# New times in the tables that order every engine's queue, and a head-by-head layout for the first pair

## The chip, the cores and the metric

The kernel runs on one core of one Trainium2 chip. The metric is the time of one launch in microseconds on the device; the time of a kernel is the median of its runs. The profile is of one execution of its own.

## The reference

Two batches of 8 heads, 768 positions, 64 wide. Each position of q and k is assigned to one of 16 clusters of its head, and attention goes only to keys of the query's own cluster. The result, 1536 tokens by 512, goes through two MLP layers of 512 to 2048 to 512.

```python
q_assign = np.argmax(np.einsum('bhsd,hcd->bhsc', q_n, c_n), axis=-1)
k_assign = np.argmax(np.einsum('bhsd,hcd->bhsc', k_n, c_n), axis=-1)
mask = q_assign[:, :, :, None] == k_assign[:, :, None, :]
scores = np.where(mask, scale * np.matmul(q, k.transpose(0, 1, 3, 2)), -1000000000.0)
...
x = softmax(scores) @ v, heads side by side as 512 columns
h = x @ w_in;  g = h * np.cos(h);  x = g @ w_out
h = x @ w_in2; g = np.where(h > 0, h, np.exp(np.minimum(h, 0)) - 1); x = g @ w_out2
```

q_n, k_n and c_n are the rows divided by their norms. q, k, v and the centroids are float32, the weights of the MLPs are float64.

## The kernel before

**Staging.** The 16 heads are worked on in eight pairs, pp = 0 to 7. A pair has 12 steps, one for each block of 128 queries of one head, 96 steps in all. In a step, qk (L741, L744) multiplies one block of queries with all 768 keys. Each operand is split into a rounded high part and the rest (low part); both are stacked along the contracted dimension in tiles X0, X1, and a second product, with the tiles T0, T1, adds the remaining term of the split together with the mask in 16 further rows, which come from Z. rowmax (L749, DVE) takes the row maximum, expo (L757, ACT) the exponential, turn (L766, PE) transposes it in six blocks, p_hi (L780, ACT) and p_lo (L786, DVE) split it, and av (L797, PE) multiplies it with the values. x_low, x_main (L839, L850, ACT) and x_add (L858, POOL) put the result into X; recip_rows and recip_out (L817, L823) send the reciprocal row sums through DRAM with DMAs on SP, and x_mul (L864, POOL) multiplies by them.

**What a pair needs before its steps.** load_nat (L300 to L319) loads k, q and v from DRAM on SP's queue: 192 KB for each head of k and q (two buffers each), 384 KB for v of both heads (one buffer). raw_pe (L436) transposes, raw_out, raw_copy and raw_low (L445 to L462) split into high and low, stack (L473 to L478) copies these with six DMAs on SP into X0, X1, T0 and T1. square and sum_sq (L530 to L552) give the squared norms, norm_seed and norm_step the norms by Newton steps, sims_pe (L581, PE) the similarities with the centroids, sims_add (L588, DVE) and sims_scale, sims_max, sims_eq, sims_first, best and assign (L601 to L647) the cluster of each position, mask_pe (L655) and mask_out (L667 to L683) the rows of the mask, which four DMAs on SP bring from the tile Z into T0 and T1 of k and q. values_hi (L699) and values_lo (L708), on POOL, split v. For the first pair first_pe, first_hi, first_low and first_hi2 (L490 to L519) stand in place of raw and stack, and norm_steps (L361 to L370, eleven small operations on DVE) in place of norm_step.

**The MLPs.** A block is (m, t, f): layer m, 512 tokens t of 3, 128 of the 2048 hidden columns f. load_w (L105 to L120) brings the weights of one f into a slot with two DMAs, w_part (L122 to L150) turns the float64 words into a rounded high part and a low part: part 0 on ACT (L133, u), part 1 a shift on DVE (L135), part 2 an or with the low word on DVE (L137), part 4 on ACT (L142), part 5 a subtract on POOL (L148). x_hi, x_lo (L171, L179) split the input tokens, g1 (L198) is the first product, act (L215 to L240) the activation in eight parts (in layer 1 with ACT's Sin at L224, the product on DVE at L226 and the low part GL on POOL at L240), g2 (L257) the second product into four accumulators, finish (L268 to L274) copies the four into X or into o, from where an output DMA goes (L278). open_mlp closes the pool of the pairs' tiles and opens the first five weight slots, close_attention opens the others.

**What sets the order.** The tables at L26 to L33 give every part a time in steps: FIRST for the first pair, PAIR for a pair before its steps (its zero is the first step of the pair ahead), STEP, HALF and UNIT for what belongs to a step, to three steps, to six; LAST for the change from attention to layer 1; MLP for blocks. All parts are collected, sorted by time, and issued in that order inside one manual schedule:

```python
with tc.manual_schedule():
    for time, _, part, args in sorted(items, key=lambda a: a[:2]):
        part(*args)
```

So each engine, and SP's queue of DMAs, runs its own instructions in the order of these times; between engines only data and free buffers are waited for. The numbers matter only through the order that they give.

Of the kernel before, what the change touches and what calls it, by code (L numbers as in the profile page):

```python
# [8 lines left out]
F32 = mybir.dt.float32  # L9
# [5 lines left out]
AF = mybir.ActivationFunctionType  # L15
ALU = mybir.AluOpType
# [24 lines left out]
SS_ON = {'k': 'pool', 'q': 'pool'}  # L41
# [13 lines left out]
def kernel(ctx: ExitStack, tc: tile.TileContext, q, k, v, centroids,  # L55
# [225 lines left out]
    with ExitStack() as actx:  # L281
# [23 lines left out]
        def load_nat(pp, which, js=(0, 1)):  # L305
            b, hp = divmod(pp, NP)
            src = {"q": q, "k": k, "v": v}[which]
            if which == "v":
                t = nat.tile([128, 2, C, D], F32, tag=which, name="nat_v")
                nats[pp, which] = t  # L310
                nc.sync.dma_start(out=t, in_=src[b, 2 * hp:2 * hp + 2].rearrange("h (p c) d -> p h c d", c=C))
            else:
                if js[0] == 0:
                    nats[pp, which] = nat.tile([128, C, 2, D], F32, tag=which, bufs=2, name=f"nat_{which}")
                for j in js:
                    nc.sync.dma_start(out=nats[pp, which][:, :, j, :],
                                      in_=src[b, 2 * hp + j].rearrange("(p c) d -> p c d", c=C))
# [688 lines left out]
```

## Time and profile before

| | us |
|---|---|
| runs | 842.17, 837.16, 836.62 |
| median of the runs | 837.16 |
| profiled execution | 839.53 |
| its span (first to last instruction) | 836.7 |
| PE busy | 790.7 |
| DVE busy | 514.2 |
| ACT busy | 484.2 |
| POOL busy | 408.5 |

The engines are PE (TensorE), DVE (VectorE), ACT (ScalarE), POOL (GpSimd) and SP, which here only issues DMAs. In a list of instructions each line has the start and the length in microseconds, the engine, the line of the kernel, the operation, the tile written and the tiles read, and in square brackets how long the engine had stood idle and what ended that: the engine, tile and line of the instruction, or the DMA. An xN behind the tile is the number of equal instructions in a row that the line stands for. PEclk is the TensorE clock that was granted, as a share of its full 2.4 GHz.

### The profile page before, as it was taken

Reading aid. Unit: us, or ns where it says so; the run is one execution under the profiler, and the core shown is the slowest. Engines: PE = TensorE matmul, PEld = TensorE weight load, DVE = VectorE, ACT = ScalarE, POOL = GpSimd, SP = SyncE. Lnnn points to the kernel's source line nnn. Section 1 sums busy time; section 2 is a strip of 40 time slices with the busy share of each in tenths; the row PEclk is TensorE's granted clock in tenths of the full one; section 3 lists DMA queues with packets and bytes.
Section 4 is the critical chain, followed back from the end, with each engine's and each line's share of the span. In section 5 each row is a group of like instructions: output and inputs, shape, how many; then the busy total and the mean of one; then the engine's idle time right before and its main releaser. Section 6 shows DMA issues by size and latency. Waiting matters only on the chain.

```text
span 836.7 us, 11270 instructions
## 1 busy us (share of the span) xinstructions
PE 790.7 (94%) x4003; PEld 671.1 (80%) x4003; DVE 514.2 (61%) x766; ACT 484.2 (58%) x894; POOL 408.5 (49%) x426
## 2 busy tenths in 40 slices
PE   5789999999998898989999999998998999999998
PEld 4689989998897686768888888876886888888886
DVE  7978998988987989985445445596675111121110
ACT  4568988988987966764333443447454333343232
POOL 3546676666662685772223222278878322212221
PEclk9689999999999999999999999999999999999999
DMA  5447467457347196000000045452000100000001
GB/s 115 106 74 165 93 141 177 88 134 171 76 97 262 18 319 243 1 0 1 1 0 1 1 152 201 155 201 97 1 1 0 51 1 0 1 36 16 0 1 50
DMA packets 65479, 67.98 MB, mean 81 GB/s; under 512 B 33488, under 2 KB 53968, under 8 KB 65424
## 3 DMA queue, kind: packets, MB, share of 16 engines
q1 hardware_dynamic: 65424, 67.28, 29.7%
q8 instruction: 31, 0.51, 0.3%
q14 instruction: 24, 0.20, 0.1%
HBM read 46.17 MB, written 3.19 MB: 59 GB/s over the span
## 4 chain that ended last, share of the span: by engine, by line
PE 58%; DVE 19%; ACT 6%; DMA 6%; POOL 6%; issue 4%; SPq 1%; POOLq 0%; ACTq 0%
PE a L257 23%; PE h L198 22%; DVE u L137 4%; PE pt L766 4%; PE px L797 3%; DVE PL L786 2%; DVE m L749 2%; POOL slot L148 2%; DMA raw<-in_moe_w_out_dram 2%; DVE u L135 2%; ACT u L133 2%; PE pt_sim L581 2%; PE s L741 2%; PE s L744 1%; DMA X1q<-lo 1%
## 5 line engine op out<-in xcount | busy, mean ns | idle before, releaser
L240 POOL TENSOR_TENSOR GL<-A,GH 128x512 fp32r<-128x512 f32 x96 | 137.1, 1428 | 279.7 <-ACT GH L235 258.8
L198 PE MATMUL h<-XH,slot 128*128 128x512 f32 x768 | 250.8, 390 | 4.3 <-POOL slot L148 4.3
L198 PEld LDWEIGHTS h<-XH,slot 128*128 128x128 f32 x768 | 144.0, 188 | 36.4 <-POOL slot L148 6.6
L198 PE MATMUL h<-XL,slot 128*128 128x512 f32 x384 | 150.0, 391 | 1.6 <-DVE XL L179 1.5
L257 PE MATMUL a<-GH,slot 128*128 128x512 f32 x384 | 125.2, 390 | 0.0
L232 DVE SCALAR_TENSOR_TENSOR A<-R,h 128x512 f32<-128x512 f32 x48 | 32.8, 684 | 145.3 <-ACT R L230 121.0
L257 PE MATMUL a<-slot,GH 128*128 128x512 f32 x384 | 119.3, 392 | 2.0 <-DVE X L270 1.9
L786 DVE TENSOR_TENSOR PL<-pt,PH 128x384 fp32r<-128x384 f32 x192 | 99.6, 550 | 19.8 <-ACT PH L780 18.3
L780 ACT ACTIVATE PH<-pt 128x384 fp32r<-128x384 f32 x192 | 87.4, 502 | 24.2 <-PE pt L766 23.8
L766 PE MATMUL pt<-ident,P 128*128 128x128 f32 x576 | 89.9, 283 | 6.7 <-DVE PL L786 3.7
L749 DVE TENSOR_REDUCE m<-s 128x1 f32<-128x768 f32 x96 | 90.8, 946 | 6.2 <-PE s L744 4.8
L757 ACT ACTIVATE P<-s,m 128x768 f32<-128x768 f32 x96 | 88.1, 918 | 7.1 <-DVE m L749 6.3
L148 POOL TENSOR_TENSOR slot<-u,slot 128x1024 fp32r<-128x1024 f32 x32 | 82.9, 2591 | 12.8 <-ACT slot L142 12.7
L257 PEld LDWEIGHTS a<-slot,GH 128*128 128x128 f32 x384 | 72.4, 189 | 17.7 <-DVE X L270 2.4
L198 PEld LDWEIGHTS h<-XL,slot 128*128 128x128 f32 x384 | 72.2, 188 | 17.7 <-DVE XL L179 2.8
L228 ACT ACTIVATE R<-h 128x512 f32<-128x512 f32 x48 | 28.4, 592 | 99.4 <-PE h L198 99.4
L257 PEld LDWEIGHTS a<-GH,slot 128*128 128x128 f32 x384 | 72.1, 188 | 15.4 <-DVE A L226 0.4
L766 PEld LDWEIGHTS pt<-ident,P 128*128 128x128 f32 x576 | 68.9, 144 | 13.8 <-DVE PL L786 6.1
L257 PE MATMUL a<-GL,slot 128*128 128x512 f32 x192 | 75.5, 393 | 3.6 <-POOL GL L240 3.6
L257 PE MATMUL a<-slot,GL 128*128 128x512 f32 x192 | 75.4, 393 | 0.7 <-POOL GL L240 0.7
L137 DVE SCALAR_TENSOR_TENSOR u<-raw,u 128x1024 uint32<-128x1024 uint32 x32 | 70.3, 2198 | 0.7
L235 ACT ACTIVATE GH<-A 128x512 fp32r<-128x512 f32 x80 | 50.1, 627 | 34.1 <-DVE A L226 24.5
(139 smaller groups left out, 1271.6 us busy)
## 6 DMA issues: line engine op xcount, KB each, us to landing
raw<-in_moe_w_in_dram SPq DMA_DIRECT2D x32, 512.0 KB, 6.1
raw<-in_moe_w_out_dram SPq DMA_DIRECT2D x32, 512.0 KB, 6.9
nat_k<-in_k_dram SPq DMA_DIRECT2D x16, 192.0 KB, 5.1
nat_q<-in_q_dram SPq DMA_DIRECT2D x16, 192.0 KB, 4.6
nat_v<-in_v_dram SPq DMA_DIRECT2D x8, 384.0 KB, 4.7
R<-row SPq DMA_DIRECT2D x32, 96.0 KB, 3.5
out_dram<-o SPq DMA_DIRECT2D x12, 256.0 KB, 2.0
X0k<-hi SPq DMA_DIRECT2D x7, 192.0 KB, 2.6
```

The lines of the kernel that those rows point to most:

```text
L137: nc.vector.scalar_tensor_tensor(out=u, in0=low, scalar=29, in1=u, op0=ALU.logical_shift_right, op1=ALU.bitwise_or)
L148: eng.tensor_tensor(out=lo, in0=f32(w_u[m, f]), in1=f32(hi), op=ALU.subtract)
L198: nc.tensor.matmul(h, lhsT=a[:, kd, :], rhs=b, start=(kd == 0 and i == 0), stop=(kd == NKD - 1 and i == 2))
L232: nc.vector.scalar_tensor_tensor(out=A, in0=R, scalar=-1.0, in1=h, op0=ALU.add, op1=ALU.max)
L235: nc.scalar.activation(out=GH, in_=A, func=AF.Copy)
L240: eng.tensor_tensor(out=GL, in0=A, in1=f32(GH), op=ALU.subtract)
L257: nc.tensor.matmul(accs[m, t][e], lhsT=a, rhs=b, start=(f == 0 and i == 0), stop=(f == NF - 1 and i == 2))
L749: nc.vector.tensor_reduce(out=m, in_=st[n]["s"][:, :, 0:HW], axis=AX.XY, op=ALU.max, negate=True)
L757: nc.scalar.activation(out=P, in_=st[n]["s"][:, :, 0:HW], func=AF.Exp, bias=st[n]["m"], accum_out=dens[u][:, j, r:r + 1])
L766: nc.tensor.transpose(pt[:, c * 128:(c + 1) * 128], st[n]["P"][:, e, c * 128:(c + 1) * 128], ident)
L780: nc.scalar.activation(out=ph, in_=pt, func=AF.Copy)
L786: nc.vector.tensor_tensor(out=pl, in0=pt, in1=f32(ph), op=ALU.subtract)
```

## The change

All the tables have new times, and with them most engines' queues have another order in places. Where the prediction speaks of an order, these entries are the ones (the tables are printed here with one entry to a line, the others left out):

```diff
 # FIRST, second dict (head 1 of the first pair)
-    'norm_steps': 0.7914,
+    'norm_steps': 1.525,
-    'sims_add:q': 0.7934,
+    'sims_add:q': 1.382,
-    'square:k': -1.0086,
+    'square:k': -20.284,
-    'sum_sq:k': -0.2561,
+    'sum_sq:k': -7.354,
-    'mask_pe': 3.8836,
+    'mask_pe': 3.799,
-    'mask_out:q': 4.085,
+    'mask_out:q': 4.427,
-    'values_lo': 2.8339,
+    'values_lo': 7.012,
...
 # PAIR
-    'raw_low:k:1': 1.5691,
+    'raw_low:k:1': 1.368,
-    'raw_pe:q:0': 2.675,
+    'raw_pe:q:0': 2.135,
-    'raw_low:q:1': 3.6687,
+    'raw_low:q:1': 4.213,
-    'stack:k': 2.2827,
+    'stack:k': 3.051,
-    'stack:q': 3.6861,
+    'stack:q': 5.0,
-    'load_nat:k': -3.9551,
+    'load_nat:k': -6.192,
-    'load_nat:q': -15.9556,
+    'load_nat:q': -0.577,
-    'load_nat:v': 8.0349,
+    'load_nat:v': -4.693,
-    'sims_pe:q:5': 5.677,
+    'sims_pe:q:5': 6.327,
-    'sims_pe:q:8': 6.6344,
+    'sims_pe:q:8': 6.039,
-    'values_lo:0': 11.4018,
+    'values_lo:0': 10.555,
-    'values_lo:1': 11.4113,
+    'values_lo:1': 9.536,
-    'mask_out': 9.2034,
+    'mask_out': 9.035,
...
 # UNIT
-    'recip_rows': 3.9065,
+    'recip_rows': 8.839,
-    'recip_out': 5.8425,
+    'recip_out': 9.063,
-    'x_add': 8.9091,
+    'x_add': 9.736,
-    'x_mul': 9.3379,
+    'x_mul': 13.628,
...
 # LAST
-    'open_mlp': (-12.2667,),
+    'open_mlp': (-11.915,),
-    'w_part:0': (-10.2061, -10.1596, -9.4684, -6.9746, -4.7605, -1.9051),
+    'w_part:0': (-9.3, -8.885, -8.673, -6.449, -5.648, -4.914),
-    'w_part:1': (-4.9214, -4.7585, -4.4517, -3.4424, -1.5263, 0.943),
+    'w_part:1': (-8.986, -7.104, -5.724, -3.249, -2.53, -2.367),
-    'g1': (2.0747, 2.3775, 5.2068, 5.8432),
+    'g1': (0.671, 1.959, 4.434, 5.707),
-    'close_attention': (5.9122,),
+    'close_attention': (6.221,),
...
 # MLP, first dict (layer 1)
-    'g2': 4.2196,
+    'g2': 4.6,
-    'late_g2:14': -0.193,
+    'late_g2:14': -0.733,
-    'finish:0': 5.1961,
+    'finish:0': 4.599,
-    'finish:1': 5.1941,
+    'finish:1': 4.016,
-    'finish:2': 4.5732,
+    'finish:2': 4.59,
-    'finish:3': 5.4814,
+    'finish:3': 4.616,
...
 # MLP, second dict (layer 2)
-    'g1': 0.8646,
+    'g1': 0.31,
-    'x_hi:0': 0.3601,
+    'x_hi:0': 1.072,
-    'x_hi:1': 0.8015,
+    'x_hi:1': 1.123,
-    'x_hi:2': 0.5952,
+    'x_hi:2': 1.51,
-    'x_hi:3': 0.5932,
+    'x_hi:3': 1.828,
-    'finish:0': 4.5752,
+    'finish:0': 4.121,
-    'finish:1': 4.7174,
+    'finish:1': 5.137,
-    'finish:2': 4.7389,
+    'finish:2': 6.206,
-    'finish:3': 5.0175,
+    'finish:3': 6.165,
...
```

Below the tables, the first pair's k and q lie in SBUF head by head, [128, 2, C, D], so that the rows of one head are 6 x 64 elements without a gap; the later pairs keep [128, C, 2, D] and are read through a rearranged view. The tile of the squares is [128, 2, C, D] for all pairs. No instruction is added or removed.

```diff
@@ -311,9 +311,10 @@
                 nc.sync.dma_start(out=t, in_=src[b, 2 * hp:2 * hp + 2].rearrange("h (p c) d -> p h c d", c=C))
             else:
                 if js[0] == 0:
-                    nats[pp, which] = nat.tile([128, C, 2, D], F32, tag=which, bufs=2, name=f"nat_{which}")
+                    t = nat.tile([128, C, 2, D] if pp else [128, 2, C, D], F32, tag=which, bufs=2, name=f"nat_{which}")
+                    nats[pp, which] = t.rearrange("p c h d -> p h c d") if pp else t
                 for j in js:
-                    nc.sync.dma_start(out=nats[pp, which][:, :, j, :],
+                    nc.sync.dma_start(out=nats[pp, which][:, j],
                                       in_=src[b, 2 * hp + j].rearrange("(p c) d -> p c d", c=C))
             for j in js:
                 made("nat", pp, which, j)
@@ -434,7 +435,7 @@
             pt = raw_pt[pp, w, half] = pt_tile("pt_raw")
             for c in range(HC):
                 nc.tensor.transpose(pt[:, c * 128:(c + 1) * 128],
-                                    t[:, half * HC + c].rearrange("p h d -> p (h d)"), ident)
+                                    t[:, :, half * HC + c].rearrange("p h d -> p (h d)"), ident)
 
         raws_sb = {}
 
@@ -487,7 +488,7 @@
             raw_pt[0, w, j] = ps
             for c in range(C):
                 o = (c % HC) * 128
-                nc.tensor.transpose(ps[0:64, c // HC, o:o + 128], nats[0, w][:, c, j, :], ident)
+                nc.tensor.transpose(ps[0:64, c // HC, o:o + 128], nats[0, w][:, j, c, :], ident)
 
         def first_parts(w, j):
             rows = lambda t, upper: (t[64:128] if upper else t[0:64]).rearrange("p (e n) -> p e n", e=2)
@@ -529,12 +530,12 @@
 
         def square(pp, w, js):
             need(*[("nat", pp, w, j) for j in js])
-            t = nats[pp, w][:, :, cols(js)]
-            sq = pre.tile([128, C, 2, D], F32, tag="sq", bufs=2, name="sq")
+            t = nats[pp, w][:, cols(js)]
+            sq = pre.tile([128, 2, C, D], F32, tag="sq", bufs=2, name="sq")
             if pp == 0 and SQ0_ON[w, js[0]] == "act":
-                nc.scalar.activation(out=sq[:, :, cols(js)], in_=t, func=AF.Square)
+                nc.scalar.activation(out=sq[:, cols(js)], in_=t, func=AF.Square)
             elif pp == 0:
-                nc.gpsimd.tensor_tensor(out=sq[:, :, cols(js)], in0=t, in1=t, op=ALU.mult)
+                nc.gpsimd.tensor_tensor(out=sq[:, cols(js)], in0=t, in1=t, op=ALU.mult)
             else:
                 nc.gpsimd.tensor_tensor(out=sq, in0=t, in1=t, op=ALU.mult)
             if pp > 0 and SS_ON[w] == "pool":
@@ -550,8 +551,7 @@
                 sss[pp] = pre.tile([128, 2, 2, C], F32, tag="ss", bufs=2, name="ss")
                 nrm[pp] = pre.tile([128, 2, 2, C], F32, tag="nrm", bufs=2, name="nrm")
             nc.vector.tensor_reduce(out=sss[pp][:, "kq".index(w), cols(js)],
-                                    in_=sqs[pp, w, js][:, :, cols(js), 0:(D if pp == 0 or SS_ON[w] == "dve" else D // 4 if SSQ == "quarter" else D // 2)]
-                                    .rearrange("p c h d -> p h c d"),
+                                    in_=sqs[pp, w, js][:, cols(js), :, 0:(D if pp == 0 or SS_ON[w] == "dve" else D // 4 if SSQ == "quarter" else D // 2)],
                                     axis=AX.X, op=ALU.add)
             made("ss", pp, w, js)
```

## Rows read from the trace of the kernel before

**Rows 1.** Busy time by stretch: stretch and length, five engines (instructions), PEclk, DMA share, GB/s

```profile
20.00:64.00 44.00, 36.14 (x197) 31.38 (x197) 36.75 (x72) 27.77 (x59) 21.85 (x34) 0.77 0.44 90
64.00:252.00 188.00, 182.89 (x1268) 171.02 (x1266) 167.54 (x323) 170.14 (x387) 129.09 (x199) 1.00 0.58 128
252.00:372.00 120.00, 106.79 (x509) 87.89 (x509) 106.37 (x121) 88.67 (x141) 79.09 (x41) 0.99 0.45 146
372.00:540.00 168.00, 168.00 (x743) 139.12 (x742) 84.40 (x104) 67.30 (x107) 41.62 (x32) 1.00 0.19 63
540.00:652.00 112.00, 105.20 (x447) 84.09 (x447) 78.65 (x66) 61.37 (x84) 86.19 (x54) 0.98 0.16 57
652.00:833.00 181.00, 180.96 (x799) 149.51 (x797) 24.80 (x36) 60.35 (x111) 43.78 (x34) 1.00 0.04 13
```

The five engines in these rows are PE, PEld (its weight loads), DVE, ACT and POOL.

**Rows 2.** Timeline of DVE from 20 to 110 us: start, length, instruction

```profile
23.41 0.94 DVE L749 TENSOR_REDUCE m<-s 128x1 f32<-128x768 f32 x1
...
25.63 1.41 DVE L367 SCALAR_TENSOR_TENSOR ny<-na,ny 128x12 f32<-128x12 f32 x1
...
30.55 0.95 DVE L749 TENSOR_REDUCE m<-s 128x1 f32<-128x768 f32 x1
...
41.82 0.95 DVE L749 TENSOR_REDUCE m<-s 128x1 f32<-128x768 f32 x1
...
51.95 0.96 DVE L749 TENSOR_REDUCE m<-s 128x1 f32<-128x768 f32 x1 [0.76 <-PE s L744]
...
64.58 0.96 DVE L749 TENSOR_REDUCE m<-s 128x1 f32<-128x768 f32 x1
...
95.83 0.96 DVE L749 TENSOR_REDUCE m<-s 128x1 f32<-128x768 f32 x1
```

**Rows 3.** Timeline of PE from 20 to 64 us

```profile
30.69 0.90 PE L766 MATMUL pt<-ident,P 128*128 128x128 f32 x3 [2.96 <-DVE sm L588]
...
44.42 0.25 PE L581 MATMUL pt_sim<-CC,X0q 128*128 128x32 f32 x1 [1.76 <-DMA X0q<-lo]
```

**Rows 4.** Timeline of SP's queue from 0 to 75 us

```profile
35.39 1.18 SPq L311 DMA_DIRECT2D nat_v<-in_v_dram  x1
36.67 0.46 SPq L473 DMA_DIRECT2D X0q<-hi  x1
```

**Rows 5.** Timeline of POOL, SP and PE from 64 to 100 us

```profile
87.95 2.27 POOL L708 TENSOR_TENSOR V<-nat_v,V 128x384 fp32r<-128x384 f32 x2
...
90.01 0.58 SPq L683 DMA_DIRECT2D T0k<-Z  x1
...
91.27 0.59 SPq L683 DMA_DIRECT2D T0q<-Z  x1
...
95.28 0.52 PE L744 MATMUL s<-T0k,T0q 80*128 80x384 f32 x2
```

**Rows 6.** DMA issues at 35, 79 and 91 us: KB, us from issue to landing

```profile
nat_v<-in_v_dram SPq DMA_DIRECT2D x1, 384.0 KB, 7.4
...
nat_v<-in_v_dram SPq DMA_DIRECT2D x1, 384.0 KB, 3.9
...
T0q<-Z SPq DMA_DIRECT2D x1, 48.0 KB, 2.2
```

**Rows 7.** Timeline of ACT from 245 to 300 us

```profile
257.69 1.12 ACT L133 ACTIVATE u<-raw 128x1024 f32<-128x1024 f32 x1 [3.05 <-DMA raw<-in_moe_w_out_dram]
```

**Rows 8.** PE's waits from 240 to 300 us: total, times, longest

```profile
PE px L797 <- ACT xt L839: 3.9, 1, 3.9
```

**Rows 9.** Two lines of DVE, 250 to 372 us: ns min/median/max, first and last start

```profile
L135 DVE TENSOR_SCALAR u<-u x16: 651/851/2894, 258.8 to 364.9; 128x1024 uint32<-128x1024 uint32 x16
...
L137 DVE SCALAR_TENSOR_TENSOR u<-raw,u x16: 1207/2049/3421, 260.3 to 366.4; 128x1024 uint32<-128x1024 uint32 x16
```

**Rows 10.** Groups by line, DVE, 250 to 372 us: busy, mean ns, idle before

```profile
L226 DVE TENSOR_TENSOR A<-h,R 128x512 f32<-128x512 f32 x14 | 9.6, 684 | 5.8 <-ACT R L224 5.8
```

**Rows 11.** PE's waits from 540 to 660 us: total, times, longest

```profile
PE a L257 <- DVE X L270: 1.9, 1, 1.9
```

**Rows 12.** Timeline of ACT from 815 to 837 us

```profile
830.96 2.64 ACT L274 ACTIVATE o<-a 128x512 f32<-128x512 f32 x4 [5.71 <-PE a L257]
```

More of the change, by code (lines that the diff above doesn't have):

```diff
@@ new lines @@
+PAIR = {'raw_pe:k:0': -1.51, 'raw_out:k:0': -0.19, 'raw_low:k:0': 0.991, 'raw_pe:k:1': 0.336, 'raw_out:k:1': 0.718, 'raw_low:k:1': 1.368, 'stack:k': 3.051, 'raw_pe:q:0': 2.135, 'raw_out:q:0': 2.557, 'raw_low:q:0': 3.139, 'raw_pe:q:1': 2.906, 'raw_out:q:1': 2.992, 'raw_low:q:1': 4.213, 'stack:q': 5.0, 'square:k': -1.323, 'square:q': 1.301, 'sum_sq:k': 2.315, 'sum_sq:q': 3.38, 'sims_add:k': 4.283, 'seed': 4.206, 'sims_add:q': 6.938, 'norms': 6.505, 'sims_scale': 7.231, 'sims_max': 7.267, 'sims_first': 7.682, 'load_nat:k': -6.192, 'load_nat:q': -0.577, 'load_nat:v': -4.693, 'raw_copy:k:0': -1.297, 'raw_copy:k:1': -32.11, 'raw_copy:q:0': 2.357, 'raw_copy:q:1': 3.368, 'best': 8.171, 'sims_eq': 7.631, 'values_hi:0': 7.986, 'values_lo:0': 10.555, 'values_hi:1': 8.189, 'values_lo:1': 9.536, 'norm_step:0': 4.292, 'norm_step:1': 4.476, 'norm_step:2': 5.647, 'norm_step:3': 6.046, 'sims_pe:k:0': 3.937, 'sims_pe:k:1': 4.03, 'sims_pe:k:2': 3.874, 'sims_pe:k:3': 4.082, 'sims_pe:k:4': 4.04, 'sims_pe:k:5': 3.856, 'sims_pe:k:6': 3.884, 'sims_pe:k:7': 3.919, 'sims_pe:k:8': 3.98, 'sims_pe:k:9': 4.093, 'sims_pe:k:10': 4.135, 'sims_pe:k:11': 3.909, 'sims_pe:q:0': 6.172, 'sims_pe:q:1': 6.734, 'sims_pe:q:2': 6.731, 'sims_pe:q:3': 6.757, 'sims_pe:q:4': 6.161, 'sims_pe:q:5': 6.327, 'sims_pe:q:6': 6.429, 'sims_pe:q:7': 6.751, 'sims_pe:q:8': 6.039, 'sims_pe:q:9': 6.704, 'sims_pe:q:10': 6.52, 'sims_pe:q:11': 6.248, 'assign': 8.45, 'mask_pe': 8.818, 'mask_out': 9.035}
@@ new lines @@
+STEP = {'qk': -0.216, 'rowmax': 0.007, 'expo': 0.849, 'turn:0': 1.984, 'p_hi:0': 2.503, 'p_lo:0': 2.594, 'turn:1': 2.143, 'p_hi:1': 2.525, 'p_lo:1': 2.763}
+HALF = {'av:0:0': 5.177, 'av:0:1': 5.605, 'av:1:0': 5.738, 'av:1:1': 7.344, 'av:2:0': 5.924, 'av:2:1': 7.099, 'av:3:0': 5.447, 'av:3:1': 5.597, 'av:4:0': 7.305, 'av:4:1': 6.973, 'av:5:0': 7.09, 'av:5:1': 5.461, 'x_main': 7.73, 'x_low': 7.528}
+UNIT = {'den_eps': 3.552, 'recip': 3.657, 'recip_rows': 8.839, 'recip_out': 9.063, 'x_add': 9.736, 'x_mul': 13.628}
```

10 lines of the change are left out of this document (3 added, 7 removed).

## Prediction

> **What bounds the kernel now.** I read the busy times by stretch first [rows 1]. Take each stretch's length less PE's busy time: PE stands idle 7.9 us of the 44 from 20 to 64 us, 5.1 of 188 in the regular attention (64 to 252), 13.2 of 120 where attention gives way to layer 1, nothing of 168 after that, 6.8 of 112 where layer 2 starts, and nothing in the last 181. The profiled execution took 839.53 us around a span of 836.7, so a new order of the same instructions has four places to win in: the first 64 us, the 5.1 us, the 13.2 and the 6.8. Everywhere else PE works without a gap. In the first of these places the granted clock is 0.77, against 1.00 and 0.99 in the next two: PE's work there is slowed as well as interrupted.
>
> Then I followed one instruction that occurs once per step, the row maximum on DVE (L749) [rows 2]. A regular pair of heads (12 steps) goes from 64.58 to 95.83: 31.25 us, or 2.60 us a step. The first pair goes from 23.41 to 64.58: 41.17 us, 9.9 more. Two gaps carry nearly all of that: from step 0 to 1 it takes 7.14 us (4.5 over a regular step), and from step 5 to 7 10.13 us (4.9 over two). What PE waited for in them is in its timeline [rows 3]: 2.96 us for the sims_add of DVE at 30.69, and 1.76 us for the DMA into X0q at 44.42.
>
> **The change part by part.** No instruction is added or removed, so each term is a wait that goes or comes.
>
> *Start, to the first row maximum (23.41).* The query's transposes now lead on PE, and ACT's and DVE's orders follow; the four loads of the first pair move the same bytes into longer rows. The trace has no case of the new order. Nearest is the 4.5 us by which the first gap exceeds a step, which an order on DVE can cost; one order more or less by a third of that is my bound, −1.5 to +1.5. I take −1, since the second head's ACT pass no longer stands ahead of the first mask.
>
> *norm_steps of head 1.* Its eleven small DVE operations (one of them is the 25.63 row of [rows 2]) stand between row maximum 0 and row maximum 1. They move behind row maximum 1, raw_low and sims_add of head 1, and PE's wait of 2.96 us for that sims_add goes with them. At most the gap closes whole, −4.5. At the other end nothing, or +2 if head 1's mask, which needs these steps, becomes late. I take −3.5: the steps now stand beside work of PE that was waiting for them, and something small is late next.
>
> *Stack of pair 1's queries.* On SP the 384-KB load of v stands between the stack of the keys and that of the queries [rows 4]: issued at 35.39, it lands 7.4 us later [rows 6], and X0q, issued at 36.67, is waited for until 44.42. The load now comes behind that stack and the next keys; raw_low and raw_pe of the queries come earlier too. Ends: −4.9 (the gap closes) and 0 (the vector work ahead of the stack was the later of the two). I take −3. Start, norms and stack together are −7.5 of the 9.9 by which the first pair is long.
>
> *Regular pairs.* The orders are nearly those of before: the similarities of the queries come later by a third of a step, x_mul later, values earlier. PE idles 5.1 us in all seven pairs [rows 1], so the best end is −5; I take −2. But one thing moves on SP: the load of the next pair's v now stands ahead of the four mask DMAs. Its buffer is single, so it waits for values_lo of this pair, which ends at 87.95 + 2.27 = 90.22; the masks were issued from 90.01 on [rows 5]. With 0.57 us of issue for the load, estimated from its neighbour of 0.59, T0q's mask goes out near 92.1 instead of 91.27. It landed 2.2 us after its issue [rows 6], at 93.5, and PE used it at 95.28: 1.8 us of slack, 1.0 left. If the masks also queue behind v's bytes, which take 3.9 us in this stage and 7.4 in the first [rows 6], T0q lands between 90.3 + 3.9 + 1.6 = 95.8 and 99.3, that is 0.5 to 4.0 us late, in six pairs (pair 7 is followed by no load): +3 to +24. I take the near end, +3, as the 3.9 is from a regular pair. Regular pairs together: +1 (−5 to +24).
>
> *Attention to layer 1.* The loads that open the MLP are no longer behind a recip_rows on SP, and the first weight pass sits a step later on ACT, so the 3.05 us that ACT stood at 257.69 for a DMA [rows 7] should go, and with it the 3.9 us for which PE waited on ACT's xt behind it [rows 8]. The weight passes of blocks 0 to 3 are pulled forward between the steps, under DVE's 5.8 us of waits for Sin [rows 10]. The whole idle time is 13.2 us, from which 9 at most could go; the least is 0, as DVE is as full as PE there (106.4 us busy against 106.8) [rows 1]. I take −4, the 3.9 of PE's wait.
>
> *Layer 2's start.* g2 of block 14 now precedes layer 2's first g1, and finish and the first x_hi and x_lo are reordered. Of the 6.8 us idle, 1.9 is one wait of PE for X [rows 11]. Ends −6.8 and, if the pulled-forward passes push the finishes, +2; I take −2, the 1.9.
>
> *Tail.* finish writes its blocks 0, 1, 3, 2. Block 2's accumulator is done ahead of block 3's, so its copy now stands behind the last one: 2.64 / 4 = 0.66 us [rows 12], +0.6. At worst this copy was hidden anyway (0), at most 0.66.
>
> *The rest.* From block 8 of layer 1 on, every engine's order is that of before but for the places named; PE is without a gap there [rows 1], so I put it at 0. The squares of the 14 later loads now run through their data in pieces of 64 elements; even if each cost 2.27 us more, what values_lo takes for as many elements [rows 5], the 32 us fit into the 59 us in which POOL is idle in the regular pairs (129 of 188 busy) [rows 1], so I put that at 0 as well; without that cover it would be the 32.
>
> Sum: −1 − 3.5 − 3 + 1 − 4 − 2 + 0.6 = −11.9. The profiled execution would become 839.5 − 11.9 = 827.6; it lies 2.4 above the median of 837.16, so for the median I say 837.2 − 11.9 = 825.3.
>
> **The rivals.**
>
> *A: DVE and POOL set the pace of the weight passes.* The same shift on DVE lasts 0.65 to 2.9 us and the same or 1.2 to 3.4 [rows 9], always the same shape: something outside stretches them, and DVE is full there [rows 1]. Then no order shortens the change-over, nor layer 2's start, where the same passes run: −4 and −2 become 0, the sum is −5.9, the time 831.3. For it: the spread. Against: ACT's 3.05 us are a wait for a DMA, not for DVE. The Trainium skill (SBUF — State Buffer, "Who interferes with whom") has a rule that speaks for this rival: a VectorE operation with two SBUF inputs and a GpSimd operation that reads SBUF lock each other out for a whole instruction. The or has two such inputs, and its spread agrees; no row shows which operation held the other. By it POOL's earlier subtracts only move DVE's wait, and the sum would again be −5.9.
>
> *B: no net change.* Each wait is followed by another. After the load of v has left, PE waits for the DVE work ahead of the stack; after norm_steps, for the mask of head 1; the weight passes give back what they took. For it: over four fifths of the span the orders are the same. Against: the two gaps of the first pair each have a named cause. The time is 837.
>
> *C: the masks are late, and the kernel is slower.* This is the upper end of the regular pairs: v's transfer takes 7.4 us, the masks stand behind it, T0q is 4.0 us late six times. The other terms are −12.9, so 837.2 − 12.9 + 24 = 848.3. It decides from 12.9 / 6 = 2.15 us a pair on, that is T0q landing after 97.4. For it: the order on SP is certain, and 1.0 us is little slack. Against: in a regular pair v took 3.9 us, and PE may run behind that point.
>
> **How the numbers follow.** Forecast 0.50 (own range 813 to 830: at the low end −1.5 − 4.5 − 4.9 − 1 − 9 − 3.7 + 0.6 = −24, at the high end the sum with the change-over at 0 and layer 2 at −1, −6.9), A 0.20, B 0.15, C 0.15. The range for 8 in 10 takes in A, B and most of the way to C, and at the low end some 2 us beyond the forecast's own: 811 to 844. About 1% is what a measurement of this kernel can tell from no change: 828.8 and 845.5. Faster: seven eighths of the forecast and a third of A, about 0.44 + 0.07, rounded to 0.52. Same: what is left of the forecast and of A, B, and a part of C: 0.34. Slower: the rest of C and a little for a price that I have missed, 0.14.
>
> **What would show it.** Row maxima 0 to 1 within 4 us and 5 to 7 within 7; PE's wait for X0q gone; pair starts still some 31.3 us apart (33 and more, with PE waiting at L744 or L741 for T0q's DMA, is rival C); ACT's wait of 3.05 us at the first weight slot under 1; PE idle under 5 us in the 112 us around layer 2's start. The forecast is wrong if the first pair still takes over 37 us, or if the regular pairs lengthen by over half a microsecond each.

## The result and the profile after

The changed kernel took 812.62 us (median of 4 runs, 810.56 to 814.47) against 838.59 for the kernel before in the same comparison (its three runs of above and a fourth, 840.02). The ratio is 0.9701, with a 95% interval of 0.9675 to 0.9727: 3% faster, 26.0 us. The profiled execution of it took 812.23 us around a span of 810.4, against 839.53 and 836.7. The forecast was 825.3 in a range of 811 to 844; the time lies inside, near the low end, and just below the 813 to 830 that I had given the forecast alone; the gain is more than twice the −11.9 us that I had summed.

The same stretches as in [rows 1], now for the changed kernel (columns as there: PE, PEld, DVE, ACT, POOL busy, then the granted clock):

```profile
20.00:64.00 44.00, 40.61 (x244) 37.80 (x244) 38.64 (x85) 34.22 (x72) 24.40 (x38) 0.96 0.44 103
64.00:252.00 188.00, 184.86 (x1277) 172.66 (x1275) 166.11 (x326) 172.31 (x392) 124.95 (x197) 1.00 0.60 147
252.00:372.00 120.00, 112.95 (x526) 93.61 (x527) 98.82 (x119) 87.16 (x133) 83.86 (x43) 0.99 0.34 113
540.00:652.00 112.00, 112.00 (x496) 92.73 (x495) 66.50 (x55) 58.64 (x84) 87.31 (x52) 1.00 0.12 42
```

These stretches hold later work than those of before, as the kernel is ahead by then. To compare equal work I cut both traces at the same instructions: row maxima 0, 12 and 84 (L749, one per step), the first ACT pass of block 14 of layer 1 (L215), and that of block 22 of layer 2 (L228). The row maxima of the changed kernel, DVE's timeline, to be laid beside [rows 2]:

```profile
23.50 0.96 DVE L749 TENSOR_REDUCE m<-s 128x1 f32<-128x768 f32 x1
26.43 0.96 DVE L749 TENSOR_REDUCE m<-s 128x1 f32<-128x768 f32 x1 [1.66 <-PE s L744]
...
40.18 0.96 DVE L749 TENSOR_REDUCE m<-s 128x1 f32<-128x768 f32 x1 [0.20 <-PE s L744]
...
46.28 0.96 DVE L749 TENSOR_REDUCE m<-s 128x1 f32<-128x768 f32 x1 [0.25 <-PE s L744]
...
58.68 0.95 DVE L749 TENSOR_REDUCE m<-s 128x1 f32<-128x768 f32 x1
...
242.24 0.95 DVE L749 TENSOR_REDUCE m<-s 128x1 f32<-128x768 f32 x1
```

Row maxima 0 to 1 now take 2.93 us instead of 7.14, and 5 to 7 take 6.10 instead of 10.13. Row maximum 84 of the kernel before, in DVE's timeline:

```profile
251.75 0.95 DVE L749 TENSOR_REDUCE m<-s 128x1 f32<-128x768 f32 x1
```

The two later marks, ACT's timeline, before:

```profile
371.01 0.67 ACT L215 ACTIVATE A<-h,cbias 128x512 f32<-128x512 f32 x1
...
686.12 0.60 ACT L228 ACTIVATE R<-h 128x512 f32<-128x512 f32 x1 [3.80 <-PE h L198]
```

and after:

```profile
355.05 0.67 ACT L215 ACTIVATE A<-h,cbias 128x512 f32<-128x512 f32 x1
...
659.22 0.60 ACT L228 ACTIVATE R<-h 128x512 f32<-128x512 f32 x1 [3.80 <-PE h L198]
```

| stretch of equal work | before | after | difference | forecast |
|---|---|---|---|---|
| to row maximum 0 | 23.41 | 23.50 | +0.1 | −1 |
| first pair (0 to 12) | 41.17 | 35.18 | −6.0 | −6.5 |
| six regular pairs (12 to 84) | 187.17 | 183.56 | −3.6 | +1 |
| pair 7 and the change-over, to block 14 of layer 1 | 119.26 | 112.81 | −6.5 | −4 |
| to block 22 of layer 2 | 315.11 | 304.17 | −10.9 | −2 |
| to the end | 150.58 | 151.18 | +0.6 | +0.6 |
| span | 836.7 | 810.4 | −26.3 | −11.9 |

So some six tenths of what I had not forecast lie at layer 2's start (8.9 us more than said), then come the regular pairs (4.6 more) and the change-over (2.5 more); the start and the first pair won 1.6 less than said. Where PE waited 1.9 us for X at layer 2's start [rows 11], its list of waits from 525 to 650 us is now empty.

The clock deserves its own look. The kernel before, by windows over the first pair and over layer 2's start:

```profile
24.00:36.00 12.00, 7.85 (x27) 5.65 (x27) 11.62 (x24) 5.39 (x13) 6.57 (x8) 0.51 0.30 73
36.00:45.00 9.00, 6.66 (x48) 5.54 (x49) 7.43 (x17) 7.30 (x15) 4.27 (x15) 1.00 1.02 220
45.00:54.00 9.00, 8.48 (x40) 8.10 (x39) 4.47 (x8) 2.69 (x6) 0.84 (x1) 0.62 0.52 79
576.00:584.00 8.00, 6.14 (x20) 4.91 (x21) 5.32 (x6) 4.16 (x6) 6.47 (x5) 0.79 0.00 0
```

From 24 to 36 us PE worked at 0.51 of its clock, that is at the lower level of 1.2 GHz nearly all the time, and again for most of 45 to 54, right where the two gaps of [rows 2] are. I had counted these gaps as waits. They were waits and slow work: in the first gap the clock had fallen before PE's wait (it was 0.70 from 21 to 24 us), and PE is busy for 8.48 of the 9 us from 45 to 54 with only 40 matmul records. Of the changed kernel only one such stretch is left:

```profile
24.00:36.00 12.00, 10.52 (x51) 9.38 (x51) 9.93 (x30) 7.50 (x17) 4.94 (x5) 1.00 0.47 117
36.00:42.00 6.00, 5.74 (x33) 5.54 (x33) 5.09 (x12) 4.97 (x9) 3.08 (x13) 0.72 1.09 228
```

### The profile page after: what moved, and what is told of

It reads as the page before. It is cut to its first block, busy times and chain, and to the rows that moved or that the text cites. A ratio compares the mean times of both kernels' runs of the same rounds, so it can differ in the third digit from the quotient of the medians.

```text
span 810.4 us, 11258 instructions
## 1 busy us (share of the span) xinstructions
PE 782.3 (97%) x4003; PEld 670.4 (83%) x4003; DVE 502.2 (62%) x766; ACT 483.6 (60%) x894; POOL 414.2 (51%) x426
## 4 chain that ended last, share of the span: by engine, by line
PE 75%; DVE 12%; ACT 8%; DMA 2%; issue 2%; SPq 1%; ACTq 0%; POOL 0%; DVEq 0%; POOLq 0%
PE a L257 31%; PE h L198 31%; DVE m L749 3%; PE pt L766 3%; PE px L797 3%; DVE PL L786 3%; ACT PH L780 2%; PE pt_sim L581 2%; ACT P L757 2%; PE s L741 2%; PE s L744 2%; DMA row<-den 1%; ACT u L133 1%; ACT slot L142 1%; DVE u L137 1%
## 5 line engine op out<-in xcount | busy, mean ns | idle before, releaser
L749 DVE TENSOR_REDUCE m<-s 128x1 f32<-128x768 f32 x96 | 91.1, 949 | 4.7 <-PE s L744 4.6
L228 ACT ACTIVATE R<-h 128x512 f32<-128x512 f32 x48 | 28.6, 597 | 103.3 <-PE h L198 100.7
L148 POOL TENSOR_TENSOR slot<-u,slot 128x1024 fp32r<-128x1024 f32 x32 | 81.3, 2541 | 11.1 <-ACT slot L142 10.8
L797 PE MATMUL px<-PH,V 128*128 128x384 f32 x192 | 68.7, 387 | 0.1
L224 ACT ACTIVATE R<-R,cbias 128x512 f32<-128x512 f32 x48 | 34.6, 722 | 52.0 <-DVE R L221 52.0
## 6 DMA issues: line engine op xcount, KB each, us to landing
nat_k<-in_k_dram SPq DMA_DIRECT2D x16, 192.0 KB, 4.1
nat_q<-in_q_dram SPq DMA_DIRECT2D x16, 192.0 KB, 3.6
X0k<-hi SPq DMA_DIRECT2D x7, 192.0 KB, 2.6
```

What stands on the lines that cost most here:

```text
L148: eng.tensor_tensor(out=lo, in0=f32(w_u[m, f]), in1=f32(hi), op=ALU.subtract)
L224: nc.scalar.activation(out=R, in_=R, func=AF.Sin, scale=-2.0 * PI, bias=cbias[:, 1:2])
L749: nc.vector.tensor_reduce(out=m, in_=st[n]["s"][:, :, 0:HW], axis=AX.XY, op=ALU.max, negate=True)
L797: nc.tensor.matmul(tx[g][:, 0:HW], lhsT=V2s[pp][:, j, c, :], rhs=halves[g][a][:, c, :], start=(n == 0), stop=(n == 2 * C - 1))
```

## The experiments

Each kernel was timed beside the kernel before on the same chip, so the ratios are to be compared, not the microseconds: the kernel before took 841.32 in the first set, 841.02 in the second and 839.50 in the third. The edits are printed against the changed kernel. The table gives for each kernel the ratio with its interval and, from one profiled execution, the stretches of above, in us, cut at the same instructions. The six pairs hardly vary between executions: 182.65 to 184.61 us in the nine profiles with the new order of the pairs (recip_back apart), 186.31 and more in the four with the old one.

| kernel | first pair | six pairs | change-over | to block 22 of layer 2 | ratio |
|---|---|---|---|---|---|
| before | 41.17 | 187.17 | 119.26 | 315.11 | 1 |
| layout_only | 39.44 | 186.31 | 121.40 | 315.05 | 0.9999 [0.9977, 1.0021] |
| new_first | 34.94 | 192.00 | 120.01 | 315.00 | 1.0005 [0.9975, 1.0036] |
| old_late | 36.49 | 184.61 | 118.92 | 315.07 | 0.9899 [0.9865, 0.9932] |
| old_mlp | 35.55 | 183.99 | 115.62 | 314.99 | 0.9839 [0.9806, 0.9871] |
| after | 35.18 | 183.56 | 112.81 | 304.17 | 0.9701 [0.9675, 0.9727] |
| old_pair | 38.99 | 194.38 | 121.41 | 303.95 | 0.9926 [0.9901, 0.9952] |
| norm_back | 34.12 | 182.65 | 113.50 | 304.10 | 0.9677 [0.9650, 0.9705] |
| v1_back | 36.52 | 182.76 | 113.81 | 304.05 | 0.9688 [0.9659, 0.9717] |
| vload_back | 33.55 | 183.29 | 112.95 | 304.08 | 0.9675 [0.9633, 0.9718] |
| recip_back | 36.52 | 239.18 | 115.92 | 304.03 | 1.0343 [1.0295, 1.0392] |
| mlp0_old | 33.58 | 183.88 | 116.74 | 311.68 | 0.9795 [0.9756, 0.9834] |
| mlp1_old | 36.49 | 183.70 | 113.64 | 319.95 | 0.9862 [0.9824, 0.9901] |
| vload_tail | 36.50 | 183.75 | 114.06 | 304.08 | 0.9687 [0.9654, 0.9720] |

**The tables, one more at a time.** The first four kernels go from before to after: the layout alone, then FIRST, then the pairs' and steps' tables, then LAST; with MLP it is the changed kernel.

layout_only (all tables of before):

```diff
-FIRST = ({'cen_sq': -71.944,
+FIRST = ({'cen_sq': -20.244,
...
```

> The tables of before with the head-by-head layout of the first pair alone. Theory (the order of the queues does it all): the time of before, 838.6 within 1.5 us, first row maximum at 23.4 within 0.5. Rival (the longer rows land sooner and start everything): 834 to 836, first row maximum before 21.5.

841.37 us against 841.32, ratio 0.9999: the theory holds. The first load is waited for 3.8 us instead of 4.3, and the first row maximum is at 24.0, no sooner than before (0.6 later, a little more than the half microsecond of the theory). Its first pair, by windows:

```profile
24.02:63.46 39.44, 34.41 (x185) 30.91 (x184) 34.08 (x67) 26.34 (x57) 19.41 (x33) 0.71 0.47 96
```

With the order of before, and the load of v still between the two stacks, row maxima 5 to 7 take 6.53 us here, not 10.13, and PE waits nowhere for X0q. PE works at a clock of 0.50 from 24 to 45 us in this execution, while in the kernel before it was back at 1.00 from 36 on and ran into that wait. So the second gap of [rows 2] comes and goes without a change of the tables.

new_first (the new FIRST, all other tables of before):

```diff
-PAIR = {'raw_pe:k:0': -1.51,
+PAIR = {'raw_pe:k:0': -1.1069,
...
```

> Layout and the new FIRST; PAIR, STEP, HALF, UNIT, LAST and MLP are those of before. Theory (the first pair is shortened by its own times): 832 to 834, first pair (row maximum 0 to 12) 35 to 37 us instead of 41.2. Rival (the gap of steps 5 to 7 is closed by pair 1's stack, which PAIR times): 835 to 836, first pair 38 to 39, with PE still waiting for X0q near row maximum 6.

840.23 us, ratio 1.0005: both were wrong. The first pair is as short as the theory said, 34.94 us, 6.2 less than before, but the next six take 192.0 instead of 187.2 and the rest goes before block 14. Two of the regular pairs, by windows:

```profile
58.70:89.42 30.72, 30.22 (x212) 28.43 (x211) 27.72 (x53) 28.18 (x66) 21.42 (x33) 1.00 0.59 135
121.09:154.92 33.83, 31.83 (x212) 29.94 (x211) 28.00 (x55) 28.40 (x66) 21.44 (x33) 0.95 0.55 124
```

The longer pair is 3.1 us longer with the same 212 matmul records: 1.5 us more idle and 1.6 more busy, at a granted clock of 0.95. What it begins with is in SP's timeline:

```profile
120.80 2.53 SPq L823 DMA_DIRECT2D R<-row  x2
...
124.54 0.49 SPq L474 DMA_DIRECT2D X0k<-hi  x1
```

SP spends 2.53 us on recip_out's two DMAs (L823), then sends the next row sums, and only then the key stack of the next pair: X0k goes out 3.45 us after the pair's row maximum at 121.09, and PE later waits 1.8 us for X1k of that stack, once in the six pairs.

old_late (LAST and MLP of before):

```diff
-LAST = {'open_mlp': (-11.915,),
+LAST = {'open_mlp': (-12.2667,),
...
```

> The changed kernel with LAST and MLP of before. Theory (pairs save 6.0 in the first and 3.6 in the next six, and nothing is given back): 829 within 1.5; the regular pairs 30.4 to 30.9 us. Rival (a shorter attention only waits for the weights at the change-over): 832 to 835, with ACT waiting longer than 5 us for the DMA of the first weight slot.

831.34 us, ratio 0.9899, that is 830.1 for a kernel before of 838.59: the theory. ACT waits for no weight DMA over 1 us there, and PE's 3.9 us for xt [rows 8] are gone too, with LAST and MLP of before. Yet the change-over takes 118.92 us, only 0.3 less than before: PE's longest wait from 240 to 300 us is now for p_lo (3.5 us in the kernel before), and blocks 0 to 14 of layer 1 take 79.7 us instead of 77.9.

```profile
PE pt L766 <- DVE PL L786: 5.9, 5, 2.5
```

old_mlp (MLP of before):

```diff
-MLP = ({'w_part:0': -0.596,
+MLP = ({'w_part:0': -0.7106,
...
```

> The changed kernel with MLP of before alone. Theory (LAST brings about 6 us, the block times of MLP the other 10): 822 to 824, PE idle 6 to 7 us again around the start of layer 2 and a granted clock below 1.00 there. Rival (the start of layer 2 runs well because the blocks before it are early): 813 to 816.

825.80 us, ratio 0.9839 (825.1 by the same reckoning), a little above the theory's range: LAST takes 3.3 us off the change-over (118.92 to 115.62), not 6, and the other 2.8 come with MLP. Layer 2's start takes 314.99 again, so the 10.9 us there belong to MLP, not to being early. PE's waits from 515 to 660 us in this kernel (total, times, longest):

```profile
PE a L257 <- POOL GL L240: 2.6, 3, 0.9
PE a L257 <- DVE X L270: 1.9, 1, 1.9
PE h L198 <- POOL slot L148: 1.8, 2, 1.3
PE h L198 <- DVE XL L179: 1.5, 1, 1.5
```

One more expectation fell: the granted clock is 1.00 there, and the stretch is still as long as before. PE idles 7.9 us from 515 to 660, and on the way to block 22 it is busy for 307.05 us against 304.17 in the changed kernel. So a lower clock is not needed for this loss.

**PAIR taken out.** old_pair (PAIR, STEP, HALF and UNIT of before):

```diff
-PAIR = {'raw_pe:k:0': -1.51,
+PAIR = {'raw_pe:k:0': -1.1069,
...
```

> The changed kernel with PAIR, STEP, HALF and UNIT of before; FIRST, LAST and MLP are new. Theory (with the order of before the regular pairs give back what the first pair saved, by waits and the lower granted clock behind them): six regular pairs about 192 us instead of 183.6, time 820 to 823. Rival (the gain was given back to LAST of before alone): regular pairs under 187, time 813 to 817.

834.48 us, ratio 0.9926. The theory's mechanism is there (six pairs 194.4 us), but the loss is twice what I expected, because the change-over is long too, at 121.4, and so is the first pair (38.99, at a clock of 0.87). PE's waits from 58 to 290 us:

```profile
PE s L741 <- ACT P L757: 8.8, 2, 6.2
PE pt_sim L581 <- DMA X1k<-lo: 4.0, 3, 1.8
```

The 8.8 us sit in the change-over: ACT has the weight passes at the places that the new LAST gives them, while the queue of before brings the weights too late. ACT stands, and PE waits for its exponential:

```profile
265.16 1.12 ACT L133 ACTIVATE u<-raw 128x1024 f32<-128x1024 f32 x1 [2.50 <-DMA raw<-in_moe_w_out_dram]
```

The pairs repeat the picture of new_first. In one that takes 30.90 us recip_out's issue is 1.14 and X0k goes out 3.4 us after the row maximum of 62.60; in one of 33.84 it is 3.44, and X0k goes out 4.1 us after that of 93.50:

```profile
63.09 1.14 SPq L823 DMA_DIRECT2D R<-row  x2
...
66.02 0.49 SPq L474 DMA_DIRECT2D X0k<-hi  x1
...
92.74 3.44 SPq L823 DMA_DIRECT2D R<-row  x2
...
97.56 0.49 SPq L474 DMA_DIRECT2D X0k<-hi  x1
```

recip_out's DMAs start only when the row sums of recip_rows have landed in DRAM (in this pair the sums land at 92.67, and the first of the two DMAs starts at 92.74), and what is behind them on SP waits with them. In the changed kernel it stands behind the key stack, which goes out 1.8 us after the row maximum (60.48 after 58.68).

**That order alone.** recip_back:

```diff
-'recip_rows': 8.839, 'recip_out': 9.063
+'recip_rows': 3.9065, 'recip_out': 5.8425
```

> The changed kernel with recip_rows and recip_out at their times of before, so that both stand ahead of the key stack on SP at a pair's start. Theory (these DMAs hold up the stack, PE waits for X1k and its clock falls behind the wait): X0k issued 3 to 4 us after a pair's first row maximum instead of 1.8, PE's waits for X1k over 2 us in sum, six regular pairs 187 to 194 us instead of 183.6, time 816 to 824. Rival (another entry of PAIR or UNIT does it): pairs under 185, time within 1.5 us of 812.6.

870.38 us, ratio 1.0343: slower than the kernel before, by 29 us as the ratio has it. The direction is the theory's, the size is not: with the later stack of the new PAIR two recip_out now stand ahead of it, where the kernel before has one. In the pair that begins at 98.54 X0k goes out 10.8 us after the row maximum:

```profile
100.35 2.46 SPq L823 DMA_DIRECT2D R<-row  x2
...
107.28 1.96 SPq L823 DMA_DIRECT2D R<-row  x2
...
109.34 0.54 SPq L474 DMA_DIRECT2D X0k<-hi  x1
```

The second of these starts 0.01 us after the row sums sent at 102.91 have landed, 4.4 us after their issue. PE's waits from 58 to 300 us in this kernel:

```profile
PE pt_sim L581 <- DMA X0k<-lo: 21.1, 6, 4.7
PE pt_sim L581 <- DMA X1k<-lo: 7.0, 6, 1.4
```

These 28 us are half of the 55.6 by which the six pairs are longer. As the dose is larger than in the kernel before, this shows the lever, not its share of the −3.6.

**My own terms undone.** norm_back:

```diff
-'norm_steps': 1.525
+'norm_steps': 0.92
```

> The changed kernel with norm_steps of head 1 put back between row maxima 0 and 1. Theory (the term of 3.5 us): row maxima 0 to 1 take 6.5 to 7.5 us instead of 2.9 and the time is 815.5 to 817. Rival (the steps are regained in the slack of the first pair): the first gap is long, the pair is not, time within 1 us of 812.6.

814.15 us, ratio 0.9677 (811.5 by the same reckoning): the rival. Row maxima 0 to 1 take 4.88 us instead of 2.93, less than the theory's 6.5 to 7.5, and yet the first pair is 34.12, no longer than in the changed kernel.

v1_back:

```diff
-"values_lo")), 0), load_nat, 1, "v")
+"values_lo")), 4.0), load_nat, 1, "v")
-'values_hi': 4.683, 'values_lo': 7.012
+'values_hi': 1.5455, 'values_lo': 2.8339
```

> The changed kernel with the first load of v for pair 1 (and the values of head 1, which must be done before it) back between the stacks of pair 1's keys and queries. Theory (the term of 3 us, the load on SP is the cause): row maxima 5 to 7 take 8.5 to 10 us instead of 6.1, PE waits for X0q, time 815 to 817. Rival (the vector work ahead of the stack was the cause): 5 to 7 under 7 us, time within 1 us of 812.6.

814.83 us, ratio 0.9688 (812.4 by the same reckoning): the rival again. The load is back between the two stacks, at 31.08 on SP, X0q goes out at 33.33 instead of 33.18, and PE does not wait for it. In this order the load does not cost the 3 us.

The two first pairs have to be read with their clock. By windows: norm_back, then v1_back:

```profile
23.67:57.79 34.12, 32.25 (x199) 29.50 (x200) 31.87 (x68) 26.41 (x57) 18.18 (x32) 1.00 0.48 113
```

```profile
23.44:59.96 36.52, 35.49 (x199) 32.88 (x200) 30.01 (x67) 26.59 (x57) 18.09 (x32) 0.91 0.45 105
```

mlp0_old has the first pair of the changed kernel as it is, vload_tail all but the place of one load of v that pair 2 uses. Their first pairs, in this order:

```profile
23.51:57.09 33.58, 31.98 (x199) 29.64 (x200) 29.82 (x68) 26.35 (x57) 18.17 (x32) 1.00 0.49 115
```

```profile
23.45:59.95 36.50, 34.31 (x198) 32.00 (x199) 30.00 (x67) 26.54 (x57) 18.16 (x32) 0.91 0.44 101
```

With the changed kernel's own 35.18 at 0.95 that is, for the engines, one order at three clocks: 33.58, 35.18, 36.50. (mlp1_old, below, has the changed kernel's first pair without any difference and took 36.49 at 0.91.) At equal clock norm_back loses 34.12 − 33.58 = 0.5 us and v1_back 36.52 − 36.50 = 0, in one execution of each.

**The masks.** vload_back:

```diff
-'load_nat:v': -4.693
+'load_nat:v': -2.95
```

> The changed kernel with the later pairs' load of v behind the four mask DMAs. Theory (the masks have slack enough on SP, 0.7 us by the changed kernel's trace): T0q is issued 0.5 us sooner, time within 1 us of 812.6, regular pairs 30.4 to 30.9. Rival (my term of +3 is really paid, in other rows): the six regular pairs 2 to 4 us shorter together, time 808.5 to 810.5.

812.49 us, ratio 0.9675; the theory. In the changed kernel SP's and PE's timelines show the delay that I had worked out:

```profile
83.27 0.39 SPq L311 DMA_DIRECT2D nat_v<-in_v_dram  x1
...
85.03 0.59 SPq L683 DMA_DIRECT2D T0q<-Z  x1
...
88.36 0.52 PE L744 MATMUL s<-T0k,T0q 80*128 80x384 f32 x2
```

T0q lands 2.6 us after its issue, at 87.6, and PE takes it at 88.36: 0.7 us to spare, and one wait of 0.5 us in all six pairs. With the load behind the masks T0q goes out 0.7 us sooner, measured from the pair's start, and the wait is gone; the six pairs are 0.3 us shorter, which is nothing that can be told.

**Layer 2's start in halves.** mlp0_old has the first dict of MLP (layer 1) from before, mlp1_old the second (layer 2). mlp0_old:

```diff
-'finish:0': 4.599, 'finish:1': 4.016, 'finish:2': 4.59, 'finish:3': 4.616
+'finish:0': 5.1961, 'finish:1': 5.1941, 'finish:2': 4.5732, 'finish:3': 5.4814
...
```

> The changed kernel with the MLP times of layer 1 of before (g2, finish, late_g2); those of layer 2 are new. Theory (finish and the last g2 of layer 1 carry the waits for X and XL, about half of the 10.9 us at layer 2's start): time 816 to 819, PE waiting for X of L270 again. Rival (layer 2's own times carry all of it): within 1.5 us of 812.6.

823.10 us, ratio 0.9795: more than the theory's half, as 3.9 us are lost in the change-over as well. PE waits for X again, for ACT's copies (L268, 1.8 us). mlp1_old:

```diff
-'x_hi:0': 1.072,
+'x_hi:0': 0.3601,
...
```

> The changed kernel with the MLP times of layer 2 of before; those of layer 1 are new. Theory (the weight passes and g1 of layer 2 carry the waits for the slot and GL, the other half): time 816 to 820, PE waiting for a slot of L148. Rival (layer 1's finish order carries all of it): within 1.5 us of 812.6.

828.99 us, ratio 0.9862. Both theories, and with them the idea of two halves that add up, were wrong: undone alone, the two cost 7.5 and 15.8 us on the way to block 22 of layer 2, undone together 10.8. PE's waits around layer 2's start in mlp1_old (515 to 670 us):

```profile
PE h L198 <- POOL slot L148: 3.2, 1, 3.2
PE a L257 <- POOL GL L240: 2.9, 4, 0.9
PE h L198 <- DVE XL L179: 2.8, 1, 2.8
PE a L257 <- ACT GH L235: 1.7, 1, 1.7
```

This is worse than either set in one piece: the order at the end of layer 1 and the one at the start of layer 2 have to fit each other. Which entries carry the 10.9 us stays open.

**The tail.** vload_tail:

```diff
-'load_nat:v': -4.693
+'load_nat:v': -2.95
...
-'finish:2': 6.206
+'finish:2': 6.15
```

> The changed kernel with v's load behind the masks and finish in the order 0, 1, 2, 3. Theory: the last copy of ACT no longer stands behind another, the span ends 0.6 us sooner after the last matmul; time 811 to 812.5, which the runs will hardly tell from 812.6. Rival (the copy was hidden by the output DMA): the stretch from the last matmul to the end is the same within 0.2 us.

814.16 us, ratio 0.9687: in time not to be told from the changed kernel, as expected. The last stretch, by windows, for the changed kernel and then for this one:

```profile
674.00:810.40 136.40, 132.06 (x583) 109.03 (x581) 19.07 (x27) 45.07 (x82) 31.07 (x24) 1.00 0.04 16
```

```profile
676.10:812.50 136.40, 132.58 (x585) 109.47 (x584) 19.08 (x27) 45.18 (x82) 31.20 (x24) 1.00 0.04 16
```

PE is without a gap until its last matmul, so what is missing to 136.4 is the tail: 4.3 us against 3.8 (3.7 in the kernel before). The theory holds. None of the kernels is clearly faster than the changed one.

## Why the prediction came out as it did

- *What bounds the kernel.* Right: all of the gain came from the four places where PE idled. Too small was the price of such a place. At the change-over and at layer 2's start I took one wait that the trace names, while the whole idle time could go, and with it some of PE's busy time.
- *The range.* Its low end, 811, held only by the margin of 2 us that stood beyond my own low end of −24. That sum had −1 for the regular pairs and −3.7 for layer 2's start, where I had worked out −5 and −6.8 as the ends; the change measured was −26. The signs that I had named all came true, but they do not show the causes: 5 to 7 within 7 us came true in layout_only too, without any new order.
- *Start.* Forecast −1, measured +0.1. The new layout and the new order of the first transposes together bring nothing.
- *norm_steps and the stack of pair 1's queries.* The sum was nearly right (−6.5 for −6.0), the steps were not. "I take −3.5" and "I take −3" fail: put back alone, the two cost 0.5 and 0 us. Both gaps of [rows 2] lie where the clock was 0.51 and 0.62; a wait of 2.96 or 1.76 us [rows 3] is not all that makes them 4.5 and 4.9 us long, and in layout_only the second closes with no new order. So near a sum from two terms that both fail is luck. That FIRST as a whole shortens the pair is shown (new_first, −6.2); which of its entries keeps PE at the higher clock is not.
- *Regular pairs.* Forecast +1, measured −3.6. The term for the masks, +3, was mis-sized: the order on SP and the 0.8 us were as worked out, but T0q landed before PE wanted it, one wait of 0.5 us. The waits for other things, −2, were about −2.9: PE's idle time in the six pairs went from 5.1 to 2.2 us (64 to 252 us holds six pairs, not the seven that I wrote). What I didn't name at all is recip_out on SP ahead of the key stack, the largest lever found (recip_back).
- *Change-over.* Forecast −4, measured −6.5. ACT's wait of 3.05 us at the first slot [rows 7] and PE's 3.9 us behind it [rows 8] are gone, as I said, but "the 3.9 of PE's wait" fails as the price: in old_late both are gone with LAST and MLP of before, and the stretch is 0.3 us shorter. LAST then brings 3.3 us, together with the shorter or on DVE (below), and MLP 2.8, with a wait of PE for a slot (L148) down from 3.5 to 1.0 us. That −4 was near is luck; which entries of the two tables do it was not taken apart.
- *Layer 2's start.* Forecast −2, measured −10.9: the largest miss, "I take −2, the 1.9". All 6.8 us of idle time went, which was my bound. Of the other 4.1 us, at which PE's busy time behind block 14 fell (455.2 to 451.0), some 1.7 are, by an estimate, the 8 us at a clock of 0.79 (8 × 0.21). But old_mlp has the same length at 1.00, so I can't say that it is the clock. So the step that failed is the size, one wait for the whole idle time and more; which of the entries win it, and why PE's busy time falls, stays open.
- *Tail.* +0.6, measured +0.6, and vload_tail takes 0.5 of it back.
- *Rival A* (DVE and POOL set the pace of the weight passes) is refuted by the change-over. Source lines of the changed kernel over its 16 passes, to be laid beside [rows 9]:

```profile
L135 DVE TENSOR_SCALAR u<-u x16: 681/735/2894, 249.6 to 348.3; 128x1024 uint32<-128x1024 uint32 x16
...
L137 DVE SCALAR_TENSOR_TENSOR u<-raw,u x16: 1208/1226/2824, 250.3 to 351.7; 128x1024 uint32<-128x1024 uint32 x16
```

The or's median fell from 2.05 to 1.23 us, and DVE's time for all 16 of them from 33.7 to 27.2 us. It goes with LAST: the median is 2.09 in old_late and 1.23 in old_mlp. Something does stretch these passes, but how often depends on the order, so the order can shorten them. The Trainium skill (SBUF — State Buffer, "Who interferes with whom") says that the issue order decides which of two conflicting operations of VectorE and GpSimd is blocked. The runs agree in so far as a new order changes how long the or takes, but no row shows which operation held the other.

- *Rival B* (no net change) is what the new FIRST does by itself: with the other tables of before its 6.2 us are gone by block 14. *Rival C* needed T0q 2.15 us late in each pair; it was late once, by 0.5.

## What to carry to other kernels

A place in which the busiest engine idles costs more than the longest wait that the trace names in it: take the whole idle time, and look at the granted clock of the stretch as well. On a queue that is served in order, look for the DMA that waits for another one's data: what stands behind it pays. A named wait that goes away has not been won yet: in old_late 3.9 us of waiting went and 0.3 us of time. And tables of times that were made together can't be split and priced one by one: here one of them alone was worth nothing, and the two halves of another, undone one at a time, cost twice the whole.

## What was not expected of the hardware

The same order of the first pair (but for that one load on SP) ran at a mean granted clock of 1.00, 0.95 or 0.91, with 33.6, 35.2 or 36.5 us. In the changed kernel and in vload_tail it fell shortly after 36 us, behind a stretch from 33 to 36 in which PE was busy 1.75 and 1.76 of 3 us; in mlp0_old, with 1.75 of 3, it did not fall, and in v1_back, with 2.18, it did. So a stretch with some idle time can, and need not, be followed by several microseconds at the lower level, and up to 3 us of the first pair in a single profile are no effect of any edit.
